# A new order table for a retention, ELU and softplus kernel on one core

## The chip, the cores and the metric

The program runs on one core of a Trainium2 chip. A core has five engines that are told apart here: TensorE (PE, with its weight loads PEld), VectorE (DVE), ScalarE (ACT), GpSimd (POOL) and SyncE (SP), which issues the transfers. Each engine works through its own list of instructions in order and waits for others by semaphores. The metric is the device time of one execution in microseconds: three runs of the kernel before have a median of 584.48 us (583.4 to 585.72).

## The reference

```python
for t in range(S):                                   # batch 2, 8 heads, S = 768, D = 64
    state = gamma * state + outer(k[t], v[t])        # gamma = 1 - 2**(-5 - head)
    y[t] = (q[t] @ state) / sqrt(D)
x = y as (1536 tokens, 512)
h = x @ moe_w_in                                     # 512 x 2048, then ELU
x = where(h > 0, h, exp(min(h, 0)) - 1) @ moe_w_out  # 2048 x 512
h = x @ moe2_w_in                                    # the same sizes, then softplus
out = (max(h, 0) + log1p(exp(-|h|))) @ moe2_w_out
```

The weights arrive as 64-bit floats, so a float32 weight is put together on the chip from two 32-bit words.

## The kernel before

The retention is done in twelve chunks of 128 tokens (j = 0 to 11, six per batch entry). The first layer works on three blocks of 512 tokens; for each it goes through 16 units of 128 hidden columns, so unit u runs from 0 to 47. Every fp32 product is made of three products of rounded parts: an operand is split into a high part (an ACT copy) and a low part (a DVE subtraction).

The program order is written out by hand as one long string, `TABLE`. A token such as `H.21` is a function and its argument; the last loop of the program calls one after the other, and with the scheduler off (`manual_schedule`) each engine gets its instructions in exactly the order in which the tokens call for them. So a token that stands too early on an engine makes that engine wait, with all that stands behind it. The tokens that matter here:

- `Lw.i` (L269, SP) loads 512 KB of raw weights. There are five raw buffers while the first layer's weights come in, so a load waits until an earlier tile has been converted. `Lb` (L204) is four transfers of 16 KB each, for the blocks of q and k of chunks 8 to 11; `Lv.j` and `Lk.j` (L183 to L186) load v and k of a chunk, and wait until the chunk two before is done with the buffer.
- `ct.i`, `cl.i` (ACT, L274 and L279), `cj.i`, `cs.i` (DVE, L284 and L293) convert weight tile i. Tiles 0 to 31 are the first layer's, from 32 on the second layer's.
- `ih.u`, `il.u` (L300 on ACT, L306 on DVE) split unit u's input weights, `oh.u`, `ol.u` its output weights, on the same lines.
- `H.u` (PE, L517) makes the hidden columns in one of two PSUM banks; `ar.u`, `ae.u` (ACT, L525 and L528), `ab.u` (DVE, L532), `gh.u` (ACT, L536), `gl.u` (DVE, L541) apply ELU and split; `R.u` (PE, L558) projects.
- For a chunk: `Tq.j`, `Tk.j` (PE transposes, L370), `tq.j`, `tk.j` (their copies; for chunks 8 to 11 they are DVE transposes, L377), `S.j` (L437), `m.j` (DVE mask, L447), `O.j` (PE, L480 or L459 to L466), `xh.j`, `xl.j` (L495 on ACT, L499 on DVE), `ST.j` (PE, L417) and `st.j` (DVE, L426 to L429), the state. From chunk 6 on `ST.j` uses the `H` bank that the last unit did not, and the next unit's `H` may start there only when `st.j` has read it.
- `gt.j` and `dv.j` (POOL, L396 and L363) multiply by the decay.

Of the kernel before, what the change touches and what calls it, by code (L numbers as in the profile page):

```python
# [23 lines left out]
Lv.1 Lk.2 Lq.3 Lq.2 dq.0 Tq.0 kc.3 Lg.0 tq.0 Tk.0 Lv.2 Tk.1 tk.0 tk.1 S.0 Lk.3 dq.1 Lv.3 Tq.1 dv.0 m.0 kc.2 ST.0 Lw.0 dv.1  # L24
tq.1 O.0 st.0 Lk.4 sp.1 S.1 xh.0 Lq.4 xl.0 Tk.2 Lw.1 m.1 ST.1 tk.2 Lw.2 Tq.3 Tq.2 st.1 O.1 tq.2 Lv.4 sp.2 tq.3 Lq.5 S.2 dv.2
xh.1 xl.1 Lw.3 dv.3 ST.2 m.2 Tk.3 tk.3 st.2 Lw.4 O.2 ct.0 sp.3 cl.0 Lk.5 cj.0 S.3 xh.2 cs.0 Lv.5 xl.2 ih.0 Tk.4 m.3 tk.4
Lg.1 ct.1 il.0 cl.1 O.3 cj.1 Lw.5 ct.2 cs.1 cl.2 few ST.3 xh.3 Lw.6 dv.4 cj.2 ih.1 xl.3 Tq.4 st.3 H.0 tq.4 sp.4 il.1 Lq.6
ct.3 cs.2 cl.3 cj.3 S.4 ar.0 Lw.7 cs.3 ih.2 H.1 ae.0 il.2 Lw.8 oh.0 m.4 ct.4 dv.5 cl.4 ab.0 ol.0 Tq.5 gh.0 O.4 cj.4 Lq.7
ar.1 gl.0 ae.1 cs.4 ct.5 H.2 cl.5 ab.1 ih.3 tq.5 xh.4 il.3 gh.1 cj.5 Lb.64 ct.6 xl.4 R.0 cl.6 cs.5 ar.2 gl.1 Lw.9 ct.7 oh.1
cj.6 ae.2 ol.1 H.3 cl.7 Lw.11 cs.6 ct.8 ab.2 ih.4 cj.7 cl.8 Lb.65 il.4 gh.2 cs.7 Tk.5 ST.4 ar.3 gl.2 Lk.6 tk.5 R.1 cj.8 oh.2  # L30
st.4 ct.9 Lw.10 cl.9 ol.2 sp.5 Lw.14 ae.3 cj.9 Lv.6 ct.11 ab.3 S.5 cs.9 gh.3 Lk.7 cs.8 oh.3 H.4 gl.3 ih.5 ol.3 cl.11 Lw.12
m.5 ct.10 cl.10 R.2 il.5 Lw.13 ar.4 cj.10 ae.4 cj.11 dv.6 cs.10 ab.4 Lb.66 ih.6 R.3 cs.11 gh.4 il.6 oh.4 Lw.16 gl.4 Lw.15
ol.4 Tk.6 H.5 tk.6 Lb.67 ct.13 cl.13 ct.12 cj.13 cl.12 cs.13 O.5 ct.14 cj.12 ar.5 oh.5 cs.12 ae.5 H.6 ol.5 Lw.17 ih.7 Lv.7
ab.5 xh.5 il.7 cl.14 xl.5 Lb.72 gh.5 ct.15 cj.14 R.4 cl.15 gl.5 ar.6 cs.14 ct.16 cj.15 ih.8 cs.15 ae.6 Lb.73 Tq.6 dv.7 cl.16
il.8 H.7 oh.6 tq.6 ct.17 ab.6 Lw.18 cl.17 ol.6 Lw.19 gh.6 Lw.20 cj.16 Lb.68 S.6 gl.6 ar.7 cs.16 ae.7 R.5 cj.17 ih.9 Lw.22
m.6 ct.18 ab.7 cl.18 il.9 H.8 gh.7 cs.17 ct.19 gl.7 oh.7 cj.18 cl.19 ol.7 ct.20 Lb.69 O.6 cs.18 ar.8 cj.19 ae.8 ih.10 cs.19
ST.6 Lw.21 Lw.23 xh.6 ab.8 R.6 Lw.24 cl.20 st.6 Lb.70 gh.8 xl.6 il.10 gl.8 cj.20 H.9 oh.8 cs.20 ct.21 ol.8 cl.21 ct.22 cj.21
cl.22 cs.21 Tq.7 ct.23 Tk.7 R.7 tq.7 ar.9 Lb.71 cj.22 tk.7 ih.11 tq.8 ae.9 il.11 gt.8 cl.23 Lw.25 ab.9 ct.24 H.10 Lw.26
cs.22 oh.9 Lv.8 cj.23 gh.9 cl.24 ol.9 Lw.27 gl.9 S.7 cs.23 ar.10 cj.24 ih.12 Lk.8 R.8 tk.8 ae.10 ct.25 m.7 cl.25 Lw.28 ct.26
ab.10 il.12 dv.8 gh.10 H.11 cs.24 oh.10 gl.10 cl.26 Lb.74 ol.10 cj.25 O.7 cj.26 ct.27 Lw.29 cs.25 ar.11 cs.26 ih.13 ae.11  # L40
il.13 Lb.75 cl.27 ab.11 ST.7 ct.28 cj.27 gh.11 R.9 st.7 Lw.30 cl.28 Lw.31 xh.7 gl.11 ct.29 Lb.76 cs.27 cj.28 cl.29 H.12 xl.7
oh.11 cs.28 ol.11 ct.30 cj.29 cl.30 tq.9 R.10 ar.12 cs.29 gt.9 Lb.77 ih.14 cj.30 ae.12 il.14 ct.31 ab.12 Lb.78 cl.31 H.13
# [10 lines left out]
st.10 gl.24 H.25 oh.24 ol.24 R.23 ar.25 ih.27 ae.25 il.27 ab.25 H.26 gh.25 oh.25 gl.25 ol.25 R.24 ar.26 ih.28 ae.26 il.28
ab.26 H.27 gh.26 oh.26 gl.26 ol.26 S.11 ar.27 ih.29 R.25 ae.27 il.29 m.11 ab.27 H.28 gh.27 oh.27 gl.27 ol.27 O.11 end yh.0.0
ar.28 yl.0.0 ih.30 ae.28 il.30 yh.0.1 ab.28 R.26 xh.11 yl.0.1 gh.28 xl.11 gl.28 H.29 oh.28 ol.28 R.27 ar.29 ih.31 ae.29
il.31 ab.29 H.30 gh.29 oh.29 gl.29 ol.29 R.28 ar.30 ih.32 ae.30 il.32 ab.30 cs.32 H.31 gh.30 oh.30 Lw.36 gl.30 cl.34 ol.30
cj.34 R.29 ar.31 ih.33 ae.31 il.33 ab.31 ct.36 cs.33 H.32 gh.31 oh.31 cw.0.0 Lw.37 gl.31 cl.35 ol.31 cw.0.1 cw.0.2 R.30
# [773 lines left out]
```

## Time and profile before

| | us |
|---|---|
| median of three runs | 584.48 |
| the profiled execution | 584.83 |
| its span, first to last instruction | 583.1 |
| PE busy in the span | 570.0 |
| DVE busy | 451.5 |
| ACT busy | 371.7 |

The 1.73 us between the profiled execution and its span lie outside the instructions. PE is busy nearly all the time, so a change that leaves PE its work can only take away stretches in which PE stands still or its clock is low.

### The profile page before, as it was taken

The page shows a single profiled execution, that of the slowest core. Times are in us where ns is not written, and L with a number is a line of the kernel's source. Part 1 is how long each engine was busy: PE and PEld are TensorE (multiplying, and loading weights), DVE is VectorE, ACT ScalarE, POOL GpSimd, SP SyncE. Part 2 cuts the span into 40 slices and gives each one's busy share as a digit, 9 for nine tenths or more (in the row PEclk, how much of TensorE's full clock was granted, in tenths as well). Part 3 has the DMA queues.
Part 4 walks back from the last instruction along what each step waited for, and adds up shares of the span by engine and source line. Part 5 has one row for each costly group of instructions (what it writes and reads, how often), then busy time and mean ns, then how long its engine had stood idle before and what let it go on. Part 6 is the DMA issues. An engine that isn't in the chain of part 4 may idle for free.

```text
span 583.1 us, 8690 instructions
## 1 busy us (share of the span) xinstructions
PE 570.0 (98%) x3236; PEld 485.5 (83%) x3236; DVE 451.5 (77%) x785; ACT 371.7 (64%) x678; POOL 28.4 (5%) x37
## 2 busy tenths in 40 slices
...
GB/s 200 245 311 212 183 264 206 143 43 60 161 38 1 2 1 36 104 42 150 210 239 232 2 0 1 1 1 2 0 1 0 110 2 0 2 0 1 0 1 108
DMA packets 75833, 48.28 MB, mean 83 GB/s; under 512 B 53520, under 2 KB 69904, under 8 KB 75792
## 3 DMA queue, kind: packets, MB, share of 16 engines
...
## 4 chain that ended last, share of the span: by engine, by line
PE 91%; SPq 3%; DMA 3%; ACT 1%; DVE 1%; issue 0%; DVEq 0%; ACTq 0%
PE psb L517 23%; PE psb L751 22%; PE psb L558 22%; PE psb L696 20%; DMA raw<-moe_w_in 3%; SPq L180 2%; PE psb L437 1%; SPq L269 1%; PE psb L466 1%; PE psb L370 0%; PE psb L417 0%; PE psb L459 0%; PE psb L480 0%; DMA out_dram<-o 0%; PE psb L474 0%
## 5 line engine op out<-in xcount | busy, mean ns | idle before, releaser
L751 PE MATMUL psb<-wo,g 128*128 128x512 f32 x576 | 142.1, 392 | 0.0
L751 PEld LDWEIGHTS psb<-wo,g 128*128 128x128 f32 x576 | 107.5, 188 | 19.5
L517 PE MATMUL psb<-x,wh 128*128 128x512 f32 x384 | 97.8, 397 | 5.6 <-DVE st L428 3.6
L517 PEld LDWEIGHTS psb<-x,wh 128*128 128x128 f32 x384 | 72.4, 191 | 22.0 <-ACT gh L536 4.0
L696 PE MATMUL psb<-op,wx 128*128 128x384 f32 x336 | 67.0, 339 | 0.0
L696 PEld LDWEIGHTS psb<-op,wx 128*128 128x128 f32 x336 | 60.2, 188 | 2.5
L306 DVE TENSOR_TENSOR wl<-wi,wh 128x512 fp32r<-128x512 f32 x48 | 33.7, 701 | 33.6 <-ACT wh L300 33.6
L721 ACT ACTIVATE hx<-hx 128x384 f32<-128x384 f32 x64 | 33.2, 520 | 37.5 <-DVE hx L717 37.4
L558 PE MATMUL psb<-gh,wh 128*128 128x512 f32 x192 | 56.4, 400 | 0.0
L558 PE MATMUL psb<-gh,wl 128*128 128x512 f32 x192 | 54.4, 390 | 0.0
L558 PE MATMUL psb<-gl,wh 128*128 128x512 f32 x192 | 54.3, 389 | 0.0
L517 PE MATMUL psb<-x,wl 128*128 128x512 f32 x192 | 52.2, 394 | 0.0
L284 DVE SCALAR_TENSOR_TENSOR cl<-cm,cl 128x512 int32<-128x512 int32 x64 | 45.2, 710 | 8.4 <-ACT cl L279 8.4
L274 ACT ACTIVATE cm<-raw 128x512 f32<-128x512 f32 x64 | 42.8, 668 | 12.0 <-DMA raw<-moe_w_in 8.0
L525 ACT ACTIVATE e<-psb 128x512 f32<-128x512 f32 x48 | 28.4, 592 | 34.4 <-PE psb L517 34.3
L536 ACT ACTIVATE gh<-e 128x512 fp32r<-128x512 f32 x48 | 30.2, 629 | 24.3 <-DVE e L532 24.3
L731 ACT ACTIVATE g<-hx 128x384 fp32r<-128x384 f32 x64 | 33.2, 520 | 18.7 <-DVE hx L725 18.6
L669 DVE TENSOR_TENSOR wo<-wo,wo 128x512 fp32r<-128x512 f32 x32 | 22.0, 687 | 29.7 <-ACT wo L665 29.7
L517 PEld LDWEIGHTS psb<-x,wl 128*128 128x128 f32 x192 | 36.6, 191 | 7.8
L279 ACT ACTIVATE cl<-raw 128x512 int32<-128x512 uint32 x64 | 42.5, 665 | 0.6 <-DVE wo L293 0.5
L558 PEld LDWEIGHTS psb<-gh,wl 128*128 128x128 f32 x192 | 36.1, 188 | 7.7
L558 PEld LDWEIGHTS psb<-gl,wh 128*128 128x128 f32 x192 | 36.0, 188 | 7.5
...
## 6 DMA issues: line engine op xcount, KB each, us to landing
...
```

The source lines that it names most:

```text
L274: nc.scalar.activation(out=m, in_=raws[i][:, :, :, 1].bitcast(F32), func=AF.Copy, scale=2.0 ** -112)
L279: nc.scalar.activation(out=l, in_=raws[i][:, :, :, 0].bitcast(U32), func=AF.Copy, scale=2.0 ** -29 * (1 - 2.0 ** -12), bias=-0.499)
L284: nc.vector.scalar_tensor_tensor(out=l, in0=m.bitcast(I32), scalar=3, in1=l, op0=ALU.logical_shift_left, op1=ALU.bitwise_or)
L306: nc.vector.tensor_tensor(out=l, in0=wf[f][o], in1=ws[u, o][0].bitcast(F32), op=ALU.subtract)
L517: nc.tensor.matmul(b, w[:, kk, :], x[:, kk, :], start=(n == 0), stop=(n == len(seq) - 1))
L525: nc.scalar.activation(out=e, in_=hb[u], func=AF.Relu, scale=-1.0)
L536: nc.scalar.activation(out=gh, in_=acts[u], func=AF.Copy)
L558: nc.tensor.matmul(acc[i], st[:, i * P:(i + 1) * P], mv, start=(fresh and p == 0), stop=(f == NF - 1 and p == 2))
L696: nc.tensor.matmul(bank_p[b], w[:, h, k], x[l][:, k], start=(start and i == 0), stop=(i == len(seq) - 1), skip_group_check=True)
L721: nc.scalar.activation(out=e, in_=e, func=AF.Softplus)
L731: nc.scalar.activation(out=t[:, 0], in_=hid[Q, c][1], func=AF.Copy)
L751: nc.tensor.matmul(sums2[s], t[:, x, i * P:(i + 1) * P], o[:, w], start=(left[s] == 0 and p == 0), stop=(left[s] == 2 * NQ - 1 and p == 2) ...
```

## The change

Only `TABLE` is different. The 1950 tokens are the same; their order is not. A line of it before and the line that holds the same token `ct.32` now:

```diff
-R.16 ol.17 ar.18 ih.20 Lb.95 ae.18 il.20 ab.18 H.19 gh.18 Lw.32 oh.18 Lw.33 gl.18 Lw.34 ol.18 Lw.35 S.9 ar.19 ih.21 R.17
-ae.19 il.21 ct.32 m.9 cl.32 ab.19 ct.33 tk.11 cl.33 H.20 oh.19 cj.32 gh.19 cj.33 ct.34 ol.19 gl.19 O.9 ct.35 ar.20 ih.22
+ct.32 R.20 cl.32 ar.22 cj.32 ih.24 ae.22 il.24 ct.33 ab.22 H.23 cl.33 oh.22 cj.33 gh.22 ol.22 ct.34 gl.22 S.10 ar.23 ih.25
```

PE's list and POOL's list are in the same order as before. SP's list is different from its 27th token (`Lw.6`) to `Lw.35`, ACT's from `ih.0` to the end of the first layer, DVE's from `cs.0` to the end of the first layer; from there on all lists agree.

On ACT near the start, where the columns are the line, the operation and its output and input, the copies of the third chunk's output and what follows stand like this before (tokens `xh.2`, `ih.0`, `tk.4`, `ct.1`, `cl.1`, `ct.2`, `cl.2`, `xh.3`, `ih.1`):

```order
L495 ACTIVATE x_234<-psb 128x4x128
L300 ACTIVATE wh<-wi_116 128x512
L387 ACTIVATE kT<-psb 128x512
L274 ACTIVATE cm<-raw 128x512
L279 ACTIVATE cl<-raw 128x512
L274 ACTIVATE cm<-raw 128x512
L279 ACTIVATE cl<-raw 128x512
L495 ACTIVATE x_234<-psb 128x4x128
L300 ACTIVATE wh<-wi_116 128x512
```

And at the same place now (`xh.2`, `tk.4`, `ct.1`, `ih.0`, `cl.1`, `xh.3`, `ct.2`, `cl.2`, `ih.1`):

```order
L495 ACTIVATE x_234<-psb 128x4x128
L387 ACTIVATE kT<-psb 128x512
L274 ACTIVATE cm<-raw 128x512
L300 ACTIVATE wh<-wi_116 128x512
L279 ACTIVATE cl<-raw 128x512
L495 ACTIVATE x_234<-psb 128x4x128
L274 ACTIVATE cm<-raw 128x512
L279 ACTIVATE cl<-raw 128x512
L300 ACTIVATE wh<-wi_116 128x512
```

The copy `xh.3`, on which the first `H` waits, now stands ahead of the conversion of the third weight tile. On DVE, likewise, `xl.2` and `m.3` stand ahead of `cs.0`.

On ACT around units 18 to 21, the first of these rows is `ae.19`, the row `x_1691` is `xh.9`, and the five L274 rows are `ct.32` to `ct.35` (the last two in one row); before:

```order
L528 ACTIVATE e<-e 128x512
L274 ACTIVATE cm<-raw 128x512
L279 ACTIVATE cl<-raw 128x512
L274 ACTIVATE cm<-raw 128x512
L279 ACTIVATE cl<-raw 128x512
L300 ACTIVATE wh<-wo_127 128x512
L536 ACTIVATE gh<-e 128x512
L274 ACTIVATE cm<-raw 128x512 x2
L525 ACTIVATE e<-psb 128x512
L300 ACTIVATE wh<-wi_119 128x512
L528 ACTIVATE e<-e 128x512
L495 ACTIVATE x_1691<-psb 128x4x128
```

Now, from `ae.19` on; the number in a name (x_1663) differs between builds:

```order
L528 ACTIVATE e<-e 128x512
L536 ACTIVATE gh<-e 128x512
L300 ACTIVATE wh<-wo_127 128x512
L525 ACTIVATE e<-psb 128x512
L300 ACTIVATE wh<-wi_119 128x512
L528 ACTIVATE e<-e 128x512
L495 ACTIVATE x_1663<-psb 128x4x128
L536 ACTIVATE gh<-e 128x512
L300 ACTIVATE wh<-wo_128 128x512
L525 ACTIVATE e<-psb 128x512
L300 ACTIVATE wh<-wi_119 128x512
L528 ACTIVATE e<-e 128x512
```

The conversions of the second layer's first tiles have left this place; `ct.32` now follows `oh.21`, three rows below the last one shown, and the next three are spread over units 22 and 23.

On SP the last transfers for the chunks, with their rows removed (-) and added (+):

```order
-L204 DMA qb<-q 32x4x32 x4
+L204 DMA qb<-q 32x4x32 x16
 L204 DMA qb<-k 32x4x32 x16
-L269 DMA raw<-moe_w_in 128x4x256 x4
 L183 DMA v<-v 128x4x64
 L185 DMA v<-v 64x4x64
 L186 DMA v<-v 64x4x64
+L269 DMA raw<-moe_w_in 128x4x256 x2
 L183 DMA k<-k 128x4x64
 L185 DMA k<-k 64x4x64
 L186 DMA k<-k 64x4x64
+L269 DMA raw<-moe_w_in 128x4x256 x2
```

`Lw.32` to `Lw.35` now stand behind `Lv.11`, and the last two behind `Lk.11` as well; `Lv.10` and `Lk.10` stand ahead of twelve small transfers that they followed.

## Rows read from the trace of the kernel before

**Rows 1.** The page's first section: busy time, share and instructions by engine

```profile
PE 570.0 (98%) x3236; PEld 485.5 (83%) x3236; DVE 451.5 (77%) x785; ACT 371.7 (64%) x678; POOL 28.4 (5%) x37
```

**Rows 2.** Waits of PE: waiter, whom for, us in total, times, longest

```profile
PE psb L517 <- DVE st L428: 3.6, 1, 3.6
```

**Rows 3.** Windows: stretch, its length, busy per engine, PEclk, DMA share, GB/s

```profile
162.38:166.00 3.62, 0.00 (x1) 0.03 (x1) 2.33 (x5) 3.27 (x7) 0.38 (x1) 0.89 0.35 79
166.00:171.46 5.46, 5.46 (x13) 4.30 (x14) 3.83 (x4) 0.11 (x1) 2.08 (x2) 0.50 0.00 0
...
87.30:122.00 34.70, 34.70 (x223) 28.52 (x222) 34.26 (x54) 27.41 (x51) 6.17 (x4) 1.00 0.59 156
```

**Rows 4.** The chain of waits, 153 to 178 us: start, length, what

```profile
153.94 7.91 DMA raw<-moe_w_in
...
165.54 0.32 DVE st L428
...
166.00 5.46 PE psb L517 x12
171.46 3.04 PE psb L558 x12
174.50 2.72 PE psb L517 x12
```

**Rows 5.** Timeline of SP and ACT, 152 to 163 us: start, length, instruction, idle before

```profile
152.36 2.04 SPq L269 DMA_DIRECT2D raw<-moe_w_in  x4
...
156.70 0.66 ACT L274 ACTIVATE cm<-raw 128x512 f32<-128x512 f32 x1 [4.26 <-DMA raw<-moe_w_in]
...
159.51 0.37 SPq L183 DMA_DIRECT2D v<-v  x1
...
161.25 0.60 SPq L183 DMA_DIRECT2D k<-k  x1
...
161.93 0.66 ACT L274 ACTIVATE cm<-raw 128x512 f32<-128x512 f32 x1 [0.86 <-DMA raw<-moe_w_in]
162.50 0.58 ACT L525 ACTIVATE e<-psb 128x512 f32<-128x512 f32 x1
```

**Rows 6.** Timeline, all engines, 23 to 30 us

```profile
23.70 1.28 DVE L447 TENSOR_TENSOR A<-psb,mask 128x512 f32<-128x512 f32 x2
...
24.44 0.68 ACT L274 ACTIVATE cm<-raw 128x512 f32<-128x512 f32 x1
...
25.85 0.27 PE L480 MATMUL psb<-A,early_v 128*64 128x128 f32 x1
...
27.36 0.66 ACT L274 ACTIVATE cm<-raw 128x512 f32<-128x512 f32 x1 [1.66 <-DMA raw<-moe_w_in]
...
28.47 0.59 ACT L495 ACTIVATE x<-psb 128x512 fp32r<-128x512 f32 x1
...
29.11 1.20 PE L517 MATMUL psb<-x,wh 128*128 128x512 f32 x4 [1.93 <-ACT x L495]
```

**Rows 7.** Timeline, PE, DVE, SP and POOL, 70 to 114 us

```profile
70.47 1.41 POOL L363 TENSOR_TENSOR v<-v,dec 128x512 f32<-128x512 f32 x1 [11.84 <-DMA v<-v]
...
70.88 1.53 DVE L306 TENSOR_TENSOR wl<-wi,wh 128x512 fp32r<-128x512 f32 x1
71.07 0.60 PE L370 MATMUL psb<-ident,q 128*128 128x128 f32 x4
...
72.34 0.68 DVE L391 TENSOR_TENSOR qT<-psb,gq 128x512 f32<-128x512 f32 x1
72.94 0.67 DVE L532 SCALAR_TENSOR_TENSOR e<-e,psb 128x512 f32<-128x512 f32 x1
...
105.48 0.42 DVE L428 TENSOR_TENSOR st<-psb,st 128x256 f32<-128x256 f32 x1
...
106.15 0.39 PE L517 MATMUL psb<-x,wh 128*128 128x512 f32 x1
```

**Rows 8.** Waits of SP, in total over the span

```profile
SPq L269 <- DVE wi L293: 107.7, 21, 67.1
```

More of the change, by code (lines that the diff above doesn't have):

```diff
@@ L23 @@
 ST.5 ST.11 sp.7 st.5 sp.6 sp.8 Tq.8 Tk.8 sp.9 Tq.9 Tk.9 sp.10 Tq.10 Tk.10 sp.11 Tq.11 Tk.11 st.11 Lq.0 Lk.0 Lk.1 Lq.1 Lv.0
[L24 to L42, printed above, removed]
@@ L53 @@
[L53 to L57, printed above, removed]
@@ new lines @@
+xh.1 xl.1 Lw.3 dv.3 ST.2 m.2 Tk.3 tk.3 st.2 O.2 Lw.4 sp.3 ct.0 Lk.5 cl.0 S.3 xh.2 cj.0 Lv.5 xl.2 Tk.4 tk.4 m.3 Lg.1 cs.0 O.3
+ct.1 ih.0 Lw.5 cl.1 il.0 few xh.3 ST.3 cj.1 dv.4 ct.2 xl.3 Tq.4 cl.2 cs.1 Lq.6 H.0 st.3 ih.1 tq.4 sp.4 Lw.6 il.1 cj.2 S.4
+ct.3 cs.2 ar.0 Lw.7 ih.2 H.1 m.4 ae.0 cl.3 il.2 ct.4 dv.5 cl.4 ab.0 cj.3 Tq.5 gh.0 O.4 Lq.7 cj.4 ar.1 cs.3 ae.1 gl.0 Lw.8
+oh.0 H.2 cs.4 xh.4 ol.0 ct.5 ab.1 ih.3 cl.5 tq.5 gh.1 il.3 R.0 Lb.64 ar.2 cj.5 ae.2 xl.4 ct.6 cs.5 cl.6 Lw.9 gl.1 oh.1 H.3
+cj.6 ct.7 ol.1 cl.7 cs.6 ab.2 ih.4 cj.7 Tk.5 Lb.65 gh.2 ST.4 il.4 tk.5 R.1 ct.8 cs.7 cl.8 st.4 Lk.6 oh.2 gl.2 sp.5 ar.3 ol.2
@@ new lines @@
+cs.17 ih.9 O.6 gl.7 ct.18 il.9 oh.7 cl.18 ol.7 ST.6 ar.8 cj.18 Lb.70 xh.6 R.6 st.6 ae.8 cs.18 ct.19 xl.6 ih.10 ab.8 Lw.22
+cl.19 Lw.21 il.10 ct.20 H.9 Lw.23 cj.19 gh.8 cl.20 gl.8 Lb.71 cs.19 cj.20 oh.8 Tq.7 cs.20 Tk.7 ar.9 R.7 Lw.24 tk.7 tq.7
+Lw.25 ih.11 ol.8 ae.9 il.11 ab.9 tq.8 H.10 ct.21 cl.21 gt.8 gh.9 cj.21 Lv.8 ct.22 gl.9 cl.22 cs.21 ct.23 S.7 cj.22 ar.10
+Lw.26 tk.8 oh.9 Lk.8 R.8 ae.10 m.7 cl.23 ct.24 ab.10 ol.9 Lb.72 dv.8 gh.10 H.11 cs.22 cj.23 ih.12 gl.10 cl.24 Lw.27 il.12
+ct.25 cs.23 O.7 ar.11 cj.24 oh.10 Lb.73 cs.24 ae.11 ol.10 cl.25 ab.11 ih.13 ST.7 Lw.28 cj.25 ct.26 Lw.29 R.9 gh.11 il.13
@@ new lines @@
+ct.32 R.20 cl.32 ar.22 cj.32 ih.24 ae.22 il.24 ct.33 ab.22 H.23 cl.33 oh.22 cj.33 gh.22 ol.22 ct.34 gl.22 S.10 ar.23 ih.25
+R.21 ae.23 il.25 ct.35 m.10 ab.23 H.24 gh.23 oh.23 gl.23 ol.23 O.10 ar.24 ih.26 ae.24 il.26 ab.24 ST.10 xh.10 gh.24 R.22
+xl.10 st.10 gl.24 H.25 oh.24 ol.24 R.23 ar.25 ih.27 ae.25 il.27 ab.25 H.26 gh.25 oh.25 gl.25 ol.25 R.24 ar.26 ih.28 ae.26
+il.28 ab.26 H.27 gh.26 oh.26 gl.26 ol.26 S.11 ar.27 ih.29 R.25 ae.27 il.29 m.11 ab.27 H.28 gh.27 oh.27 gl.27 ol.27 O.11 end
+yh.0.0 ar.28 yl.0.0 ih.30 ae.28 il.30 yh.0.1 ab.28 R.26 xh.11 yl.0.1 gh.28 xl.11 gl.28 H.29 oh.28 ol.28 R.27 ar.29 ih.31
@@ new lines @@
+c.7.1 s.7.3 yl.1.5 yh.1.6 n.7.1 bh.9 j.7.3 M.8.1 yl.1.6 s.7.1 M.8.2 vh.7.3 bl.9 u.0 wh.16 Q.7.0 j.7.1 sh.9 c.8.0 vh.7.1
+vl.7.3 vl.7.1 M.8.6 n.8.0 wl.16 s.8.0 M.8.5 sl.9 u.1 j.8.0 Q.7.1 cw.10.1 vh.8.0 cw.10.0 vl.8.0 M.8.7 wh.17 wl.17 Q.7.2 u.2
+c.8.2 n.8.2 s.8.2 M.8.4 o.0.3 o.0.4 o.0.5 d.0.4 M.8.3 c.8.3 d.0.3 j.8.2 bh.10 d.0.5 n.8.3 Q.7.3 c.8.1 s.8.3 bl.10 vh.8.2
+sh.10 n.8.1 M.9.1 j.8.3 o.0.0 vl.8.2 o.0.2 d.0.0 M.9.2 o.0.1 s.8.1 d.0.2 sl.10 u.0 d.0.1 vh.8.3 Q.8.0 wh.18 j.8.1 c.9.0
+vh.8.1 vl.8.3 vl.8.1 M.9.6 n.9.0 wl.18 s.9.0 M.9.5 cw.11.1 u.1 j.9.0 Q.8.1 cw.11.0 vh.9.0 vl.9.0 M.9.7 wh.19 wl.19 Q.8.2 u.2
@@ new lines @@
+c.9.2 n.9.2 s.9.2 M.9.4 j.9.2 M.9.3 vh.9.2 c.9.3 vl.9.2 bh.11 Q.8.3 n.9.3 c.9.1 s.9.3 n.9.1 bl.11 sh.11 s.9.1 M.10.1 j.9.3
+wh.20 j.9.1 vh.9.3 M.10.2 wl.20 u.0 vh.9.1 vl.9.3 Q.9.0 c.10.0 vl.9.1 n.10.0 sl.11 s.10.0 M.10.6 j.10.0 cw.12.1 vh.10.0
+M.10.5 cw.12.0 u.1 vl.10.0 Q.9.1 M.10.7 wh.21 wl.21 Q.9.2 u.2 c.10.2 n.10.2 s.10.2 M.10.4 j.10.2 M.10.3 vh.10.2 c.10.3
+vl.10.2 bh.12 Q.9.3 n.10.3 c.10.1 s.10.3 n.10.1 bl.12 sh.12 s.10.1 M.11.1 j.10.3 wh.22 j.10.1 vh.10.3 M.11.2 wl.22 u.0
+vh.10.1 vl.10.3 Q.10.0 c.11.0 vl.10.1 n.11.0 sl.12 s.11.0 M.11.6 j.11.0 cw.13.1 vh.11.0 M.11.5 cw.13.0 u.1 vl.11.0 Q.10.1
```

135 lines of the change are left out of this document (68 added, 67 removed).

## The prediction

> **What bounds the kernel now.** I read the page's busy times first. TensorE is busy for 570.0 of 583.1 us [rows 1], and its list is the same in both kernels, so what can go is the 13.1 us in which it stands still, and stretches of low clock. The waits of TensorE come next, to split those 13.1 us: the longest single one is 3.6 us, before an `H`, for the state copy at L428 [rows 2]; the first `H` waits 1.93 us for the copy at L495 [rows 6]; the rest lies in the first 27 us and at the end, when the last outputs leave, where the lists agree. From 29.11 us to 162.38 us TensorE has no idle time at all, and none from 166.00 us until the last outputs.
>
> The windows around the long wait show what it costs. From 162.38 to 166.00 us TensorE does nothing, and from 166.00 to 171.46 us, where it is busy throughout, the granted clock is 0.50, so 1.2 instead of 2.4 GHz [rows 3]. The chain of waits has the same place by pieces: twelve matmuls of L517 take 5.46 us and the next twelve of L558 3.04 us, where the next piece of twelve takes 2.72 us [rows 4].
>
> The chain also names the cause. It goes from the state copy back to a load of `moe_w_in` that takes 7.91 us [rows 4]. In the timeline SP issues four such loads in a row from 152.36 us on; ACT then stands idle for 4.26 us before the first conversion at 156.70 us, and for another 0.86 us before the fourth, at 161.93 us; only then comes `ar.20`, at 162.50 us [rows 5]. These are `ct.32` to `ct.35`, weights of the second layer that nothing asks for yet. They stand on ACT ahead of `ar.20`, and DVE's `ab.20`, `tq.11` and `st.9` stand in this order behind that; `H.21` needs the bank that `st.9` reads. So it isn't the weights that TensorE lacks; ACT's list puts a landing in front of work that is due.
>
> **The change, term by term.** The sum is made against the profiled execution, 584.83 us, which is 0.35 us above the median of 584.48 us.
>
> First, the stall at 162 us. `ct.32` now follows `oh.21`. Without the wait, `H.21` starts where TensorE fell idle. What goes is the idle time, 3.62 us [rows 3], and the half clock: 5.46 - 2.72 = 2.74 us and 3.04 - 2.72 = 0.32 us [rows 4]. Together 6.68 us.
>
> What is late next there? `Lw.32` now stands behind `Lv.11`, which has to wait for `ST.9`: it was issued at 159.51 us and its three parts took until 161.25 us [rows 5]. TensorE will be some 2 us earlier (below), so `Lw.32` is issued at about 161.25 - 2.0 = 159.2 us. The first of the four loads took 156.70 - 152.36 = 4.3 us to its conversion [rows 5], the last 7.91 us [rows 4]; two at a time should be nearer the first, so it lands between 163.5 and 167.1 us. `ct.32` is reached when `H.21` is through its ELU. `H.21` would start at 162.4 - 2.0 = 160.4 us and end at 163.1; `ar`, `ih`, `ae`, the DVE step, `gh` and `oh` behind it are six steps of about 0.6 us [rows 5, 7], so 166.8 us. If the load is late it is so by 0.3 us, and queued behind `ct.32` is `ar.22`, which is due only when `H.22` ends, at about 168.5 us. I cost it at nothing; what hides it is `R.20` on TensorE, and without this cover each us of lateness would still have `R.21` in front of TensorE. The four loads moved past `Lv.11` and `Lk.11` let these be issued earlier, and nothing else stands behind them on SP until the middle of the second block. `Lv.10` and `Lk.10` go past twelve small transfers and may hold these up by a wait for chunk 8; they serve chunk 11, whose score is two chunks away: nothing.
>
> Second, the start. `H.0` waited for `xh.3`, which stood behind `ct.2` on ACT; `ct.2` waited 1.66 us for its load until 27.36 us, and `xh.3` came at 28.47 us, although TensorE had finished its input, the last matmul of L480, at 25.85 + 0.27 = 26.12 us [rows 6]. Now `xh.3` stands ahead of `ct.2`. On DVE `m.3` has one step less in front of it, 0.60 us from start to start [rows 7]; it began at 23.70 us [rows 6], so the matmuls behind it end at about 25.5 us. On ACT `ct.1` waits for its load; it began at 24.44 us [rows 6], and I keep that. Then come `ct.1`, `ih.0` and `cl.1`, about 0.55 us each from start to start, so `xh.3` runs from 26.1 to 26.7 us and `H.0` starts at 26.8 us. That is 2.3 us before 29.11 us. `S.4` and `H.1` follow on TensorE; `ct.3` now stands in front of `ar.0`, but its use comes two units later. Gross gain 2.3 us.
>
> Third, what hands on the 2.3 us. Every engine that feeds TensorE must be 2.3 us earlier for the whole of the first block, and DVE is busy for 34.26 of 34.70 us between 87.30 and 122.00 us [rows 3]: it has nothing to give but its order. In the new list the DVE steps for which TensorE waits have fewer conversions ahead of them: `tq.6` 79 steps instead of 84, `st.7` 132 instead of 136, `ab.12` 143 instead of 148. Four steps of 0.60 us are 2.4 us, about what is needed. The tightest place I found is `H.12`: it started at 106.15 us, and `st.7` had read its bank at 105.48 + 0.42 = 105.90 us [rows 7], 0.25 us before. In the new order: `Tq.6` ended on TensorE at 71.07 + 0.60 = 71.67 us [rows 7], now at 69.4 us, and `tq.6` follows at once; from `tq.6` (72.34 us) to `st.7` (105.48 us) lie 33.14 us and 52 steps [rows 7], now 53, so `st.7` comes at 69.4 + 33.14 + 0.64 = 103.2 us and has read the bank at 103.6 us. `H.12` is due at 106.15 - 2.3 = 103.85 us. It fits by 0.25 us; each further us that DVE loses is lost at `H.12`. Bounds of the term: 0, if DVE gives nothing back, and 2.3 us; a loss below 0 is a rival. I take 2.0 us, near the upper end, since the row by which it fits is nearer than any that speaks for a loss.
>
> One thing in that row of DVE can be different. A step `il.8` took 1.53 us at 70.88 us, beside a POOL multiplication that ran from 70.47 us for 1.41 us, where the DVE step behind it, which reads PSUM, took 0.68 us [rows 7]. The Trainium skill (SBUF — State Buffer, section "Who interferes with whom") says why: a DVE instruction with two SBUF inputs contends with a GpSimd instruction that reads SBUF, and the one that comes second waits. By this rule the new order would be worse at `gt.8`: POOL begins it when `tq.8` ends, and the next DVE step is now a conversion with two SBUF inputs instead of one from PSUM; a full 0.85 us (1.53 - 0.68) instead of about half of that makes `H.12` 0.2 us late, and with one more such meeting 1.0 us. That is a rival of its own below.
>
> The sum: 584.83 - 6.68 - 2.0 = 576.15, so 576.2 us.
>
> **Rivals.**
>
> Both gains, forecast: 575.2 to 577.6 us. Chance 0.56.
>
> The start's gain is lost in the DVE-bound stretch, since conversions, each four to five steps later, come late for some unit and TensorE waits in pieces too short to lower its clock (the 1.93 us at 29 us were followed by no lower clock). Time 584.83 - 6.68 = 578.2 us. For it: DVE's share in that stretch. Against: the steps in question moved by the right amount. 0.16.
>
> DVE and POOL meet oftener: 576.15 + 1.0 = 577.2 us. 0.07.
>
> A new wait as long as the old one, at another place. ACT still waits in its order for landings, and a gap of 3.62 us brings the half clock with it. Then 6.68 us are handed back: 576.15 + 6.68 = 582.8 us. For it: the old order had one such place. Against: from 29 to 162 us and from 166 us on no row has one, and most tokens moved by a few steps. Half of the chance for a smaller wait of about 3 us, 579 us. 0.10.
>
> The change does not do what it says: `ct.32`'s wait goes but `H.21` still waits for `st.9`, say behind `tq.11`, whose blocks come by the reordered small transfers. With the 2.3 us lost too this is no change, 582 to 585 us. Against: SP issued these before 152.36 us [rows 5], with more than 5 us to spare. 0.06.
>
> Slower: the ring of five raw buffers. SP waits for conversions on DVE for 107.7 us in total [rows 8], so a load is issued only when an older tile is converted. If each conversion is five steps later, 3.0 us, the load behind it is 3.0 us later, then its conversion, and so on: the 16 loads of the first layer's second half go three times round the ring, 9 us. From the point where more than about 3 us of that reach the weights of units 12 to 15, TensorE waits; 9 us idle and 3.06 us of half clock make 576.15 + 12.1 = 588.2 us. Against: ACT and DVE order put the conversions only as much later as loads had waited before. 0.05.
>
> **How the numbers follow.** A time within 0.5% of 584.48 us, 581.6 to 587.4 us, can't be told from no change in a measurement like this. Faster: forecast 0.56, lost start 0.16, POOL 0.07, and the half of the new wait that is small, 0.05: 0.84. Same: 0.05 and 0.06, so 0.11. Slower: 0.05. The range of 8 in 10 begins at 574.6 us, below the forecast by the 1.1 us by which runs of the kernel before differ from their median and the 0.3 us that I kept back at the start, and ends at 581.3 us, which takes in the lost start and the smaller new wait. The likeliest case alone has 575.2 to 577.6 us.
>
> **What would show it.** In the new trace: no idle time and no 0.50 of the granted clock near 160 us, with `H.21` following `R.18` directly; `xh.3` near 26.1 us and the first L517 matmul near 26.8 us; `H.12` within 0.3 us of the matmuls ahead of it; TensorE's busy time some 3 us less than 570.0 us, its half-clock part. A wait of TensorE of over 1 us between 30 and 170 us, above all for `st` or for a split of weights, or a first `H` after 28 us, would make the forecast wrong.

## The result, and the profile after

The new order takes 576.49 us in the median of four executions (575.93 to 578.05), the old one 585.10 us beside it (583.4 to 586.14): a ratio of 0.986, with a 95% interval of 0.9828 to 0.9892. The forecast was 576.2 us, the range 574.6 to 581.3 us. The profiled execution took 576.78 us, 8.05 us less than that of before.

The page's head after: span and instructions, busy time by engine, and the granted clock of TensorE in 40 slices, in tenths.

```profile
span 575.1 us, 8682 instructions
PE 568.2 (99%) x3236; PEld 484.8 (84%) x3236; DVE 451.9 (79%) x785; ACT 371.7 (65%) x678; POOL 27.9 (5%) x37
PEclk9999999999999999999999999999999999999999
```

The work is the same as in [rows 1]. Where the 8.0 us of the span went is seen by cutting both spans at the same three instructions: the first `H`, `H.21`, and `R.46`. Windows of before (stretch, its length, busy time and instructions of PE, PEld, DVE, ACT and POOL, granted clock, DMA share, GB/s):

```profile
0.00:29.11 29.11, 23.92 (x269) 18.03 (x269) 16.89 (x29) 10.71 (x18) 9.98 (x22) 1.00 1.04 222
29.11:166.00 136.89, 133.27 (x904) 108.27 (x905) 116.53 (x190) 101.40 (x183) 16.32 (x15) 1.00 0.65 173
166.00:324.31 158.31, 158.31 (x805) 130.59 (x805) 125.71 (x200) 114.35 (x207) 2.08 (x2) 0.98 0.30 94
324.31:583.10 258.79, 254.49 (x1261) 228.57 (x1260) 192.38 (x369) 145.24 (x273) 0.00 (x0) 1.00 0.04 13
```

And after, cut at the same instructions:

```profile
0.00:27.26 27.26, 25.07 (x269) 19.28 (x269) 15.47 (x27) 9.52 (x16) 8.99 (x21) 1.00 1.10 227
27.26:161.26 134.00, 133.19 (x904) 108.46 (x905) 118.63 (x191) 98.72 (x178) 17.88 (x15) 1.00 0.60 159
161.26:316.67 155.41, 155.41 (x805) 128.47 (x804) 123.16 (x198) 116.88 (x211) 1.04 (x1) 1.00 0.37 112
316.67:575.10 258.43, 254.49 (x1261) 228.60 (x1260) 194.61 (x373) 146.61 (x275) 0.00 (x0) 1.00 0.04 13
```

The lengths differ by 1.85, 2.89, 2.90 and 0.36 us. In the second stretch TensorE's time without work (length less busy) falls from 3.62 to 0.81 us. In the third it has none in either kernel; there the same 805 matmuls take 2.90 us less, and the mean clock is 1.00 instead of 0.98. That is the half-clock part of [rows 3]. The last stretch was given no work in another order, and its matmuls take 254.49 us in both kernels. Its 0.36 us lie behind the last output transfer, which is issued here, before and after (start, length, queue, line, operation, output and input, count):

```profile
579.72 0.34 ACTq L767 DMA_DIRECT2D out_dram<-o  x1
```

```profile
572.08 0.35 ACTq L767 DMA_DIRECT2D out_dram<-o  x1
```

The transfer lands 2.1 us after its issue in both, but the span ends 3.4 us after it before and 3.0 us after it now. All other traces of this document part in the same way: 3.4 us in the five that keep the old order from the 179th token on, apart from single tokens, and 3.0 us, in one 3.1 us, in the six that have the new one there. So this gain comes with the order, but no run shows by what.

The waits of TensorE after (engine, line, released by: us in total, times, longest), the answer to [rows 2]:

```profile
PE psb L240 <- DVE warm L234: 1.3, 1, 1.3
PE psb L370 <- DVE early L360: 0.7, 1, 0.7
PE psb L517 <- DVE st L428: 0.6, 1, 0.6
PE psb L437 <- DVE qT L391: 0.2, 1, 0.2
PE psb L517 <- ACT x L495: 0.2, 1, 0.2
```

The wait of 3.6 us for the state is gone; one of 0.6 us for another state is there, which before didn't have. The place where the stall was, on TensorE, ACT, DVE and SP after (start, length, engine, line, operation, output and input, shape, count, idle time before), against [rows 4, 5]:

```profile
160.17 0.40 DVE L428 TENSOR_TENSOR st<-psb,st 128x256 f32<-128x256 f32 x1
160.35 1.07 PE L558 MATMUL psb<-gl,wh 128*128 128x512 f32 x4
161.26 1.98 PE L517 MATMUL psb<-x,wh 128*128 128x512 f32 x8
162.15 1.10 SPq L269 DMA_DIRECT2D raw<-moe_w_in  x2
...
167.71 0.67 ACT L274 ACTIVATE cm<-raw 128x512 f32<-128x512 f32 x1
```

`H.21` follows `R.18` with no bracket, at 161.26 instead of 166.00 us. The load `Lw.32` is issued at 162.15 us, and the conversion `ct.32` at 167.71 us has no bracket either: the load was there when ACT came to it.

### The profile page after: what moved, and what is told of

It is laid out like the page before. It is cut to its first block, busy times and chain, and to the rows that moved or that the text cites. A ratio compares the mean times of both kernels' runs of the same rounds, so it can differ in the third digit from the quotient of the medians.

```text
span 575.1 us, 8682 instructions
## 1 busy us (share of the span) xinstructions
PE 568.2 (99%) x3236; PEld 484.8 (84%) x3236; DVE 451.9 (79%) x785; ACT 371.7 (65%) x678; POOL 27.9 (5%) x37
## 4 chain that ended last, share of the span: by engine, by line
PE 89%; DVE 5%; ACT 2%; DMA 2%; issue 1%; DVEq 0%; ACTq 0%
PE psb L751 23%; PE psb L696 21%; PE psb L558 20%; PE psb L517 20%; PE psb L437 2%; PE psb L370 1%; DVE cl L284 1%; DVE wl L306 1%; DMA raw<-moe_w_out 1%; PE psb L417 1%; DVE wi L293 1%; ACT wh L300 1%; DMA early<-q 1%; DVE wo L293 1%; DVE A L447 1%
## 5 line engine op out<-in xcount | busy, mean ns | idle before, releaser
L517 PE MATMUL psb<-x,wh 128*128 128x512 f32 x384 | 96.0, 392 | 0.8 <-DVE st L428 0.6
L517 PEld LDWEIGHTS psb<-x,wh 128*128 128x128 f32 x384 | 71.5, 188 | 16.5 <-ACT cl L279 1.0
L517 PE MATMUL psb<-x,wl 128*128 128x512 f32 x192 | 51.3, 389 | 0.0
L274 ACT ACTIVATE cm<-raw 128x512 f32<-128x512 f32 x64 | 42.6, 665 | 5.1 <-DVE wi L293 2.9
L284 DVE SCALAR_TENSOR_TENSOR cl<-cm,cl 128x512 int32<-128x512 int32 x64 | 43.8, 693 | 2.0 <-ACT cl L279 1.9
L517 PEld LDWEIGHTS psb<-x,wl 128*128 128x128 f32 x192 | 36.1, 188 | 7.5
```

Source lines behind the costliest of these rows:

```text
L274: nc.scalar.activation(out=m, in_=raws[i][:, :, :, 1].bitcast(F32), func=AF.Copy, scale=2.0 ** -112)
L284: nc.vector.scalar_tensor_tensor(out=l, in0=m.bitcast(I32), scalar=3, in1=l, op0=ALU.logical_shift_left, op1=ALU.bitwise_or)
L517: nc.tensor.matmul(b, w[:, kk, :], x[:, kk, :], start=(n == 0), stop=(n == len(seq) - 1))
```

## The experiments

Each changes `TABLE` alone; the diffs show tokens. In the experiments' kernels all line numbers are one lower than in the two kernels (`H` has L516 instead of L517), apart from the first, which is the new kernel itself. Times are medians; each comparison is with the kernel before on the same chip.

**The new order again**, as the reference for the runs beside it.

> The new order, unchanged, beside the three that follow, since they are compared with it. 576 to 577 us; H.0 near 27.2 us, a wait of some 0.6 us at H.12.

Six executions: 576.81 us (576.4 to 577.4), ratio 0.9858 (0.9833 to 0.9883). The profiled one took 576.4 us, its span is 574.7 us. Its timeline of TensorE at the scores of chunk 3, at `H.0`, at `R.18` and at `R.46`:

```profile
21.21 1.16 PE L437 MATMUL psb<-early_v 64*128 64x128 f32 x16
...
26.84 1.20 PE L517 MATMUL psb<-x,wh 128*128 128x512 f32 x4 [0.18 <-ACT x L495]
...
158.01 1.20 PE L558 MATMUL psb<-gh,wh 128*128 128x512 f32 x4
...
316.27 1.09 PE L558 MATMUL psb<-gh,wh 128*128 128x512 f32 x4
```

This trace is the better one to set against that of before. There the scores of chunk 3 begin at 21.20 us, here at 21.21 us, in the first trace after at 22.24 us. The microsecond is lost by TensorE between 5 and 9 us. These are the same three matmuls, in the first trace and in this one:

```profile
6.05 1.49 PE L240 MATMUL psb<-warm 128*128 128x512 bf16 x3
```

```profile
5.58 0.81 PE L240 MATMUL psb<-warm 128*128 128x512 bf16 x3
```

The matmuls of L370 around them take 1.09 and 1.92 us in the first trace and 0.63 and 1.10 us here. It isn't the loads: DVE's first two steps on them begin at 4.33 and 7.95 us there, at 4.28 and 7.85 us here. The profile gives a granted clock of 1.00 for 5.1 to 9.2 us in both, so why the same work takes longer is not shown. I call this a slow beginning; it is in three more traces below, one of them with the old start. With the same beginning, `H.0` is 2.27 us earlier than before, `R.18` 1.36 us (159.37 to 158.01 us) and `R.46` 8.04 us (324.31 to 316.27 us). With the 0.36 us at the end that is 8.40 us of the span.

**Only the conversions moved.** The old order, with `ct.32` to `ct.35` and what belongs to them where the new order has them.

```diff
-ae.19 il.21 ct.32 m.9 cl.32 ab.19 ct.33 tk.11 cl.33 H.20 oh.19 cj.32 gh.19 cj.33 ct.34 ol.19 gl.19 O.9 ct.35 ar.20
+ae.19 il.21 m.9 ab.19 tk.11 H.20 oh.19 gh.19 ol.19 gl.19 O.9 ar.20
...
+oh.21 gl.21 ol.21 ct.32 R.20 cl.32 ar.22 cj.32 ih.24 ae.22 il.24 ct.33 ab.22 H.23 cl.33 ...
```

> The order before, with one thing done: the conversions ct.32 to ct.35, cl.32, cl.33, cj.32 and cj.33 of the second layer's first weights stand where the new order has them (from behind oh.21 on); transfers and start as before. Theory (ACT's list puts a landing in front of ar.20): the 3.62 us of idle TensorE and the half clock behind it go, 6.7 us, so about 578 us; H.0 at 29.1 us as before. Rival (the order of the transfers is what mattered, four loads at once behind the small ones): the stall stays, 584 to 585 us.

Twelve executions: 579.52 us (577.58 to 583.54), ratio 0.992 (0.9896 to 0.9945). `H.21` stands directly behind `R.18` here too:

```profile
160.73 1.07 PE L557 MATMUL psb<-gl,wh 128*128 128x512 f32 x4
161.63 1.98 PE L516 MATMUL psb<-x,wh 128*128 128x512 f32 x8
```

From `R.18` to `R.46` the trace takes 158.26 us (158.78 to 317.04 us), 6.68 us less than before. So moving these tokens on ACT and DVE, with the loads left in their place on SP, is enough to take the stall away. `H.0` came at 27.81 us and not at 29.1 us as expected; this trace has a slow beginning. The gain in the medians, 4.9 us, is less than the 6.68 us of the trace. The executions scatter over 6 us, and the profiled one was the fastest of them (577.58 us, one wait of 0.5 us for a state, at `H.17`). The slower ones show a mean clock down to 0.992, the fastest 1.000; a further stall in some of them would look so, but they were not profiled.

**Only the loads issued earlier.** The old order with its conversions in their old place, and the four loads ahead of `Lb.90`.

```diff
 xh.8 tq.10 gh.16 R.14
+Lw.32 Lw.33 Lw.34 Lw.35
 Lb.90 xl.8 gt.10 st.8 ... H.19 gh.18
-Lw.32 oh.18 Lw.33 gl.18 Lw.34 ol.18 Lw.35
+oh.18 gl.18 ol.18
```

> The order before, with only the four loads Lw.32 to Lw.35 issued earlier, ahead of the small transfers Lb.90; the conversions keep their place ahead of ar.20. Theory (it is the landing that ACT waits for, not the work of the conversions): the loads land before 152 us, ct.32 begins at about 152.4 us, the six ACT steps of 0.6 us fit before H.20 ends at 157.5 us, and the stall goes as in the first experiment, about 578 us. Rival (the conversions themselves are too much work at this place): ar.20 still comes some 3 us late or more, and TensorE still waits for st.9; 581 to 585 us.

Twelve executions: 585.14 us (583.68 to 587.51), ratio 1.0008 (0.9984 to 1.0033): the expectation failed. The timeline of SP, ACT, DVE and TensorE in this kernel:

```profile
151.88 8.51 SPq L203 DMA_DIRECT2D qb<-k  x16
154.54 0.67 ACT L273 ACTIVATE cm<-raw 128x512 f32<-128x512 f32 x1
...
161.86 0.71 DVE L376 STREAM_TRANSPOSE kT<-qb 128x512 f32<-128x512 f32 x1 [5.22 <-DMA qb<-k]
...
163.18 1.28 ACT L273 ACTIVATE cm<-raw 128x512 f32<-128x512 f32 x2 [4.98 <-DVE cl L283]
...
167.86 1.61 PE L516 MATMUL psb<-x,wh 128*128 128x512 f32 x3 [3.27 <-DVE st L427]
```

`ct.32` no longer waits, as intended. But the last sixteen 16 KB transfers of k are now issued from 151.88 to 160.39 us, before from 144.78 to 152.27 us, and DVE stands 5.22 us at `tk.11` for them. Of the 8.1 us some 1.8 us stood there already ahead of the four loads (the eight small transfers directly ahead of them begin at 134.04 instead of 132.22 us); the loads' own issues take 2.03 us, the transfers of v and k behind them wait 3.0 us for the loads to land, by the waits of SP, and the sixteen issues take 8.51 instead of 7.49 us. Behind `tk.11` on DVE are the conversions that free ACT's buffers, so ACT stands for 4.98 us, and `H.21` waits 3.27 us, much as before (3.62 us). The wait has changed its landing and kept its place.

**The same, with that landing out of the way.** As the last one, and `tk.11` behind `ol.20` on DVE.

```diff
-cl.32 ab.19 ct.33 tk.11 cl.33 H.20
+cl.32 ab.19 ct.33 cl.33 H.20
...
-xl.9 H.21 oh.20 ol.20 dv.11
+xl.9 H.21 oh.20 ol.20 tk.11 dv.11
```

> The second experiment again (four weight loads issued ahead of Lb.90, conversions left ahead of ar.20), with tk.11 moved on DVE from between ct.33 and cl.33 to behind ol.20, where the new order has it, so that DVE doesn't stand there for the small transfers that are now late. Theory (any engine that stands at a landing ahead of due work makes the same stall; take away both and it goes): no wait of ACT or DVE of over 1 us there, H.21 follows R.18, about 578 us. Rival (the conversions' own work is too much at this place): H.21 still waits 1 us or more for st.9.

Six executions: 579.11 us (577.87 to 579.73), ratio 0.9911 (0.9883 to 0.9939). ACT in this kernel, with the conversions where they were, ahead of `ar.20` (L524), and `H.21`:

```profile
153.81 0.66 ACT L273 ACTIVATE cm<-raw 128x512 f32<-128x512 f32 x1
...
157.38 1.22 ACT L273 ACTIVATE cm<-raw 128x512 f32<-128x512 f32 x2
159.04 0.60 ACT L524 ACTIVATE e<-psb 128x512 f32<-128x512 f32 x1 [0.44 <-PE psb L516]
...
163.69 1.98 PE L516 MATMUL psb<-x,wh 128*128 128x512 f32 x8
```

`ar.20` waits for TensorE now and not TensorE for it. The eight steps of the conversions cost nothing at this place; what cost was a landing, on either engine, in front of due work.

**The conversions put back into the new order**, and the loads ahead of `Lv.11`.

```diff
-ae.19 Lb.91 m.9 ab.19 H.20 gh.19 oh.19 Lb.92 gl.19 ol.19 Lb.93 O.9 ar.20
+ae.19 Lb.91 Lb.92 Lb.93 Lb.94 Lb.95 Lw.32 Lw.33 Lw.34 Lw.35 il.21 ct.32 m.9 cl.32 ab.19 ct.33 cl.33 H.20
+gh.19 oh.19 cj.32 cj.33 ct.34 gl.19 ol.19 O.9 ct.35 ar.20
```

> The new order, with the four loads Lw.32 to Lw.35 put back ahead of Lv.11 and their conversions back ahead of ar.20. The small transfers are issued some 6 us later in the new order than before (Lw.31 at 110.4 instead of 103.7 us), so the loads land later too. Theory (TensorE's wait is set by the landing): ACT stands at ct.32 until about 163 us, at ct.35 until 168, H.21 starts near 172 instead of 161.3 us, with the half clock behind it: 576.5 + 11 + 3, so about 590 us. Rival (the conversions' own work is what delays ar.20, whenever they land): the old price, about 583 us.

Six executions: 590.14 us (588.73 to 591.61), ratio 1.0097 (1.0066 to 1.0127). ACT's wait at `ct.32`, and two windows, TensorE's gap and what follows it:

```profile
163.01 0.66 ACT L273 ACTIVATE cm<-raw 128x512 f32<-128x512 f32 x1 [11.85 <-DMA raw<-moe_w_in]
```

```profile
161.09:172.47 11.38, 0.01 (x1) 0.03 (x1) 5.51 (x10) 7.82 (x14) 0.97 (x1) 0.60 0.78 217
172.47:178.00 5.53, 5.53 (x15) 4.38 (x16) 3.25 (x4) 0.41 (x1) 1.48 (x2) 0.59 0.01 1
```

The same tokens in the same place make the stall again, longer since the small transfers are issued later in this order. Taken out of the old order it goes, put into the new one it comes.

**Only the start.** The first 178 tokens of the new order (the same tokens as the first 178 of the old one), then the old order.

> The new order for the first 178 tokens (until R.0 and the first splits of unit 1), the order before from there on. The stall at 162 us stays. Theory (the gain at the start is handed on only where DVE's later order lets it): H.0 starts 1.8 to 2.3 us earlier, but st.7 has 136 DVE steps before it as before, so H.12 waits for it by 1 to 1.8 us, and at most 0.9 us is left: 584 us or a little over, against 585. Rival (a start that is earlier by 1.9 us is earlier all the way): 583 us, no wait at H.12.

Twelve executions: 584.47 us (581.69 to 586.89), ratio 0.999 (0.9967 to 1.0013). TensorE's waits for states:

```profile
PE psb L516 <- DVE st L427: 6.5, 3, 4.2
```

`H.0` starts at 27.45 us, and nothing of it arrives: the three waits are 1.26 us at `H.12`, 1.08 us at `H.17` and 4.20 us at `H.21`. The profiled execution was the slowest of the twelve, 586.89 us. The old middle takes the gain back at each state.

**The start and the conversions, with the old middle.** The last one with the conversions moved as in the first experiment.

```diff
 (the first 178 tokens of the new order, then of the old:)
-ae.19 il.21 ct.32 m.9 cl.32 ab.19 ct.33 tk.11 cl.33 H.20 ... ct.35 ar.20
+ae.19 il.21 m.9 ab.19 tk.11 H.20 ... ar.20 ... ol.21 ct.32 R.20 cl.32 ...
```

> The order before with both gains put in by hand: the first 178 tokens of the new order, and the conversions ct.32 to ct.35 where the new order has them; in between the DVE and SP order of before. Theory (the middle of the new order is needed to hand the start's gain on, since with the old one H.12 and H.17 wait for st.7 and st.8): no stall at 162 us, waits of 1.3 us at H.12 and some 1 us at H.17; about 578 to 579 us. Rival (only these two places matter): 576.5 us as the new order.

Twelve executions: 578.9 us (577.15 to 584.1), ratio 0.9918 (0.9894 to 0.9942), the time of the conversions alone. The profiled one, of 581.63 us, waits 0.69 us at `H.12` and 2.88 us at `H.17`; the matmul there and the window behind it:

```profile
138.79 1.47 PE L516 MATMUL psb<-x,wh 128*128 128x512 f32 x4 [2.88 <-DVE st L427]
```

```profile
138.79:142.00 3.21, 3.21 (x9) 2.54 (x10) 1.79 (x3) 0.00 (x0) 0.31 (x1) 0.60 0.38 77
```

So the old middle has a second place, `st.8` before `H.17`, with little to spare. In the kernel with only the start `H.17` was due at 137.34 us and waited 1.08 us, here it was due at 135.91 us and waited 2.88 us: TensorE came 1.43 us earlier and started no earlier. The clock stayed at 1.00 behind the shorter wait (138.42 to 142.00 us), and behind the longer one the matmuls ran in part at the lower level, 0.60 in the mean. The new order has no wait there. Its middle is what lets the start's gain through.

**The new order with the old start.** The first 178 tokens of the old order, then the new one.

> The order before for the first 178 tokens, the new order from there on. Theory (the start is worth what H.12 lets through, about 1 us): H.0 a good 1 us later than in the new order, no wait at H.12, no stall at 162 us; 0.5 to 1.3 us above the new order. Rival (the start's gain is 2 us, as summed): 2 us above it.

Six executions: 578.11 us (577.43 to 580.38), ratio 0.9885 (0.9857 to 0.9913), 1.3 us more in the median than the new order beside it. In the two profiled spans (576.7 and 574.7 us) it is 2.0 us. `H.0`, `H.12` and `R.18` in this kernel:

```profile
28.72 1.20 PE L516 MATMUL psb<-x,wh 128*128 128x512 f32 x4 [0.83 <-ACT x L494]
...
106.94 0.93 PE L516 MATMUL psb<-x,wh 128*128 128x512 f32 x3 [0.59 <-DVE st L427]
...
160.04 1.20 PE L557 MATMUL psb<-gh,wh 128*128 128x512 f32 x4
```

I had expected `H.12` not to wait when TensorE comes later; it waits 0.59 us as with the new start (0.57 us in the run beside it). `tq.6` begins some 0.2 us after TensorE has made `Tq.6` in both kernels, and `st.7` comes 34.4 us later in both, so with a later TensorE `st.7` is later too; the wait belongs to what stands between the two on DVE. The start's gain goes through it: against the run beside it `H.0` is 1.88 us later, `H.12` 2.06 us and `R.18` 2.03 us (160.04 to 158.01 us).

**The meeting of DVE and POOL avoided.** In the new order POOL begins `gt.8` when `tq.8` ends; `tq.8` now stands directly ahead of `tk.8` and `m.7`, so that the next DVE steps are a transpose that reads one operand and two that read PSUM.

```diff
-ab.9 tq.8 H.10 ct.21 cl.21 gt.8 gh.9 cj.21 Lv.8 ct.22 gl.9 ... Lw.26 tk.8 oh.9 Lk.8 R.8 ae.10 m.7 cl.23
+ab.9 H.10 ct.21 cl.21 gh.9 cj.21 Lv.8 ct.22 gl.9 ... Lw.26 tq.8 tk.8 oh.9 Lk.8 R.8 ae.10 m.7 gt.8 cl.23
```

> The new order with one token moved: tq.8 stands directly ahead of tk.8 and m.7 on DVE, so that POOL's gt.8 runs beside steps that read PSUM or have one input, not beside gl.9 and conversions. Theory (the wait of 0.58 us at H.12 comes from gl.9, which took 1.78 us instead of 0.68 beside gt.8): no DVE step beside gt.8 takes over 1 us, st.7 is about 1.1 us earlier, the wait at H.12 is gone, 0.5 to 0.8 us less than the new order in the trace; too little for the times to tell with certainty. Rival (DVE's queue of conversions sets st.7 whatever runs beside it): the wait stays at 0.4 to 0.7 us.

Six executions: 576.07 us (575.75 to 576.27), ratio 0.9845 (0.982 to 0.987), 0.74 us below the new order beside it. DVE and POOL in the new order (first trace):

```profile
91.73 1.58 POOL L396 TENSOR_TENSOR qT<-qT,gq 128x512 f32<-128x512 f32 x1 [22.52 <-DVE qT L377]
92.08 1.78 DVE L541 TENSOR_TENSOR gl<-e,gh 128x512 fp32r<-128x512 f32 x1
...
104.71 0.42 DVE L428 TENSOR_TENSOR st<-psb,st 128x256 f32<-128x256 f32 x1
105.28 1.39 PE L517 MATMUL psb<-x,wh 128*128 128x512 f32 x5 [0.58 <-DVE st L428]
```

And here:

```profile
92.03 0.68 DVE L540 TENSOR_TENSOR gl<-e,gh 128x512 fp32r<-128x512 f32 x1
...
94.68 1.31 POOL L395 TENSOR_TENSOR qT<-qT,gq 128x512 f32<-128x512 f32 x1 [25.18 <-DMA v<-v]
95.06 0.65 DVE L446 TENSOR_TENSOR A<-psb,mask 128x512 f32<-128x512 f32 x1
...
104.20 0.42 DVE L427 TENSOR_TENSOR st<-psb,st 128x256 f32<-128x256 f32 x1
104.84 1.54 PE L516 MATMUL psb<-x,wh 128*128 128x512 f32 x6
```

The step `gl.9` takes 0.68 instead of 1.78 us, the step beside POOL's multiplication 0.65 us, and `H.12`'s wait is gone. This trace has a slow beginning, so the first trace after is the one to set beside it: `R.18` starts at 157.87 instead of 158.41 us, although `H.0` came 0.28 us later. Each of the six times is below each of the six of the new order beside it.

**Two attempts to start earlier still**, on top of the last one. First `xh.3` ahead of `cl.1`, `xl.3` ahead of `cj.1`, `tq.4` ahead of `st.3`:

```diff
-ct.1 ih.0 Lw.5 cl.1 il.0 few xh.3 ST.3 cj.1 dv.4 ct.2 xl.3 Tq.4 cl.2 cs.1 Lq.6 H.0 st.3 ih.1 tq.4
+ct.1 ih.0 Lw.5 xh.3 cl.1 il.0 few ST.3 xl.3 cj.1 dv.4 ct.2 Tq.4 cl.2 cs.1 Lq.6 H.0 tq.4 st.3 ih.1
```

> The last kernel, and at the start xh.3 ahead of cl.1 on ACT, xl.3 ahead of cj.1 and tq.4 ahead of st.3 on DVE. Theory (the first H waits for xh.3 behind cl.1, and S.4 for tq.4 behind st.3): H.0 0.4 to 0.5 us earlier, no wait at S.4, and with DVE freed at gt.8 all of it is handed on past H.12: 1.0 to 1.4 us less than the new order. Rival (the next landing or H.12 takes it back): 0.5 to 0.8 us less, as the kernel before.

Six executions: 576.11 us (575.01 to 577.94), ratio 0.9846 (0.9815 to 0.9876). The first `H` no longer waits, but now the score matmuls of chunk 4 do, for `st.3`, which reads their bank and stands behind `tq.4`:

```profile
PE psb L436 <- DVE st L427: 0.8, 1, 0.8
```

So not the forecast 1.0 to 1.4 us came but the 0.7 us of the rival, the gain of the kernel before it.

Then the same with `st.3` ahead of `tq.4`, and `cs.1` and `ih.1` behind both:

```diff
+ct.1 ih.0 Lw.5 xh.3 cl.1 il.0 few ST.3 xl.3 cj.1 dv.4 ct.2 Tq.4 cl.2 Lq.6 H.0 st.3 tq.4 cs.1 ih.1
```

> The new order with tq.8 moved as before, xh.3 ahead of cl.1 on ACT, xl.3 ahead of cj.1 on DVE, and cs.1 now behind st.3 and tq.4, so that neither the bank nor the operand of S.4 is late. Theory: H.0 0.3 to 0.5 us earlier than with tq.8 alone for the same state of the first loads, no wait of TensorE at S.4 nor at H.12; 575.5 us. Rival (cs.1, now later, makes ih.1 or H.1 late and takes it back): 576.1 us, a wait at H.1.

Six executions: 576.51 us (575.61 to 577.75), ratio 0.987 (0.9844 to 0.9896). The profiled one has the shortest span seen, 573.5 us, with `H.0` at 26.19 us; `H.1` waits 0.24 us for its weights, the sign that the rival named. The intervals of the last three kernels overlap almost wholly; the times don't tell them apart. The order with `tq.8` moved is the one that scatters least, and the only one better than the new order both by its trace and by its times on one chip.

## Why the prediction was right

**The stall at 162 us** was summed as 3.62 us of idle time and 3.06 us of half clock, 6.68 us. From `R.18` to `R.46` just this was gained, in the first trace (7.64 - 0.96) and in the second (8.04 - 1.36). The cause named, ACT's list with a landing in front of due work, was shown by taking the conversions out of the old order and by putting them back into the new one. One side of it I had too narrow: it is not ACT alone. With the loads early, DVE's `tk.11` did the same by another landing.

**What is late next there** came out as nothing, as costed, though by other numbers. `Lw.32` was to be issued at 159.2 us, and went at 162.15 us, since SP came to the small transfers later; `H.21` was to start at 160.4 us and did at 161.26, so ACT came to `ct.32` at 167.71 instead of 166.8 us. The load was there; how much was to spare the trace doesn't say.

**The start** was the weaker term. Forecast were `H.0` at 26.8 us, 2.3 us gross, and 2.0 us kept. With the same beginning as before `H.0` comes at 26.84 us, 2.27 us gross, and 1.36 us arrive at `R.18`. So in this pair the gross gain was right, and the mis-sized term is what is kept. One pair is thin for it: in the four traces with the old start and no slow beginning `H.0` comes at 28.57 to 29.11 us, in the four with the new start at 26.54 to 27.45 us, 1.93 us apart in the mean. In slow beginnings it is less, 27.81 us with the old start and 27.26 and 27.54 us with the new.

The new order with the old start parts the term. It comes to `R.18` 2.03 us later than the new order, so the start is worth all of the 2.0 us forecast. But in these traces it also comes there 0.67 us later than the old order does with the same start (160.04 against 159.37 us). This is what the new middle costs by itself, and 2.03 - 0.67 gives the 1.36 us. The step that failed is "It fits by 0.25 us": the middle was taken to cost nothing. `H.12` waited 0.58 us (0.57 us in the second trace); in the first:

- `tq.6` was to start at 69.4 us. `Tq.6` ended at 70.06 us, and `tq.6` started at 70.28 us, behind a step of DVE that was still running.
- From there `st.7` came 34.43 us later, not 33.78 us as summed. `gl.9` alone was 1.10 us longer than where it stands alone; before, the step beside `gt.8` was 0.52 us longer (1.20 instead of 0.68 us).
- With `tq.8` moved the same run is 33.62 us (70.58 to 104.20 us), and `H.12` doesn't wait.

That is the rival "DVE and POOL meet oftener" in part: it was given 0.07 and 1.0 us, and taking the meeting away was worth 0.74 us in the medians. The Trainium skill (SBUF — State Buffer, section "Who interferes with whom") states that a DVE instruction with two SBUF inputs contends with a GpSimd instruction that reads SBUF. The trace agrees with it at this place: `gl.9` with two SBUF inputs began 0.35 us behind POOL's step and took 1.78 us, and a mask from PSUM beside the same POOL step took 0.65 us. The prediction misread which step differs. The one directly behind `tq.8` has two SBUF inputs in both orders; it began 0.22 us ahead of POOL's step in both and took 0.65 us. It is the next one that read PSUM before (`ab.9`, 0.68 us) and is `gl.9` now. The forecast had counted about half of 0.85 us for the meeting, and the whole of it only in a rival.

Another 0.23 us were lost at the score matmuls of chunk 4, which waited for `tq.4`'s copy; this wait I hadn't looked for. With 0.57 us at `H.12` that is 0.80 of the 0.91 us that did not arrive. The time came out at 576.49 us all the same because 0.36 us fell away at the end, behind the last output, which no term of the sum had: 584.83 - 6.68 - 1.36 - 0.36 = 576.43 us, and the second trace's execution took 576.4 us. That these 0.36 us made up for somewhat over half of what the start's term lacked is luck. Undoing the start costs 1.3 us in the medians and 2.0 us in the profiled pair.

**TensorE's busy time** was to fall by some 3 us and fell by 1.8 us in the first trace. Behind `H.21` it is 2.90 us less, as said; ahead of `H.0` the same 269 matmuls show 1.15 us more. In the second trace the busy time up to `H.0` is 23.71 us for 268 matmuls (23.92 us before), and in all it is 566.8 us, 3.2 us less than before. So the 1.15 us belong to the slow beginning and not to the order.

**The rivals.** A lost start with a time of 578.2 us is what the old middle would have made of it (578.9 us); the new middle kept most of it. The new long wait, the late `tq.11` and the ring of raw buffers didn't come: no wait beyond 27 us is longer than 0.58 us. The new wait's price was of the right kind: in the new order with the conversions put back, a gap of 11.4 us, with low clock behind it, cost 13.3 us (590.14 against 576.81 us, the two on different chips). The range's lower end is by its own terms 576.15 - 1.1 - 0.3, so 574.75 and not 574.6 us; nothing hangs on it.
